# Attention and two expert layers on one core: inputs laid out ahead of the launch, soft-expert products and loads in another order

## The chip, the cores and the metric

The kernel runs on one core of a Trainium2 chip. The metric is device microseconds of one execution, the median of several runs. The engines are TensorE (PE; PEld are its weight loads), VectorE (DVE), ScalarE (ACT), GpSimd (POOL) and SyncE (SP), which here only issues DMAs. On-chip memory has 128 partitions.

## The reference

Three layers follow each other. Attention works on chunks of 32 queries with 16 keys of left context, 8 of right context and 8 memory keys per head:

```python
for c in range(nc):                       # B, H, S, D = 4, 8, 768, 64
    q_c = q[:, :, 32*c:32*c+32]
    k_full = concat([mem_k, k[:, :, 32*c-16:32*c+40]])   # cut at the ends of the sequence
    v_full = concat([mem_v, v[:, :, 32*c-16:32*c+40]])
    a = exp(s - max(s)); a = a / (sum(a) + 1e-9)         # s = scale * q_c @ k_full.T
    out[:, :, 32*c:32*c+32] = a @ v_full
# soft layer: x is [3072, 512], 8 experts with 4 slots each
logits = x @ phi
d = softmax of logits over the tokens; slot_input = d.T @ x
for e in range(8):
    slot_out[e] = relu(slot_input[e] @ w1[e]) @ w2[e]    # w1 512x1024, w2 1024x512
x = (softmax of logits over the slots) @ slot_out
# last layer: noisy top-2 of 8 experts for each token, the same shapes of w1 and w2
out = sum over the two experts of weight * (relu(x @ w1[e]) @ w2[e])
```

## The kernel before

There are three stages: attention (0 to about 153 us), the soft layer (to about 206 us) and the top-2 layer (to the end). The change is in the first two.

**Attention** (`attention`, L1067) runs 32 steps; step i = 2u + s is half s (12 chunks) of unit u, a pair of heads of one batch. The order of the work is written by hand: a loop over i for most steps, and the list ORDER (L44) for the last four together with the dispatch of the soft layer. Step i of the loop issues, in this order: scores of step i+1 (qk, L1177, 24 small matmuls), their maximum (mx, L1190), transposes of Q or K of a later unit (tr, L1153, six transposes and four ACT copies, L1163), subtraction (sub, L1198) and exponential (L1203, ACT), the shift of V (L1135), transpose of the probabilities (at, L1208) and its copy (atc, L1214, ACT), products with V of step i-1 (av, L1223), normalization (nrm), the V load of step i+3 (L1117), a zero piece of the output (L233) or a weight piece (L161), the copies of memory values (mem_rows, L1130, POOL), parts of the logits (L1260 to L1277), and a transpose of the finished tokens of step i-2 (xt, L1246) with its copy (xtc, L1253, DVE). Q and K come from memory in their own layout (L1102) and are turned on PE; `fill_mem` (L1142) puts the memory keys between them. V comes twice a step, one transfer for each head, to 32 partitions, in runs of 64 values; `shift` copies its context to the next 32 partitions, one head on DVE and one on POOL. V has four buffers, K two. Every load waits on SP's queue, which issues in order, until its buffer has been read.

**Weights of the soft layer.** Matrices 0 to 15 are w1 and w2 of the eight experts in turn, 2 MB each, loaded in four pieces of 512 KB. `home` (L142) gives each its place: 0 and 1 in two tiles of their own, the rest in the large tile `big`, whose columns also hold the attention buffers (called arena) and the tokens xs. Matrices 0 to 3 are loaded during attention (`load_piece`); 4 to 10 are issued behind it, each when its place has been read, and 11 to 15 from within the soft stage (`next_load`, L205). Behind these come the first two matrices of the last layer (`first_load`, L216), into the place of matrices 0 and 1.

**Soft stage** (`soft`, L244). For each expert: first products (L258, 16 matmuls into PSUM p1), clearing hz (POOL, L263), relu (ACT, L264), two transposes (L267), a DVE copy into hz (L268), second products (L272, accumulated over all experts in po). Behind it stands the preparation of the last stage: `bounds` (L241) reads the first w2 of the last layer, and the routing uses the soft output.

Of the kernel before, what the change touches and what calls it, by code (L numbers as in the profile page):

```python
# [19 lines left out]
NMEM = 8  # L20
# [7 lines left out]
E = 8  # L28
SL = 32
KB_W = 40 * NCH + 24  # L30
VC = 130
# [95 lines left out]
def tile_kernel(ctx, tc, q, k, v, mem_k, mem_v, phi, sw1, sw2, wg, wn, noise, mw1, mw2, cf_in, c16_in, out):  # L127
# [14 lines left out]
    home = [*raw, *home[7:9], *home[3:7], *home[0:3], *home[7:9], *home[3:6]]  # L142

    with ExitStack() as sctx:
# [28 lines left out]
        with ExitStack() as actx:  # L173
# [4 lines left out]
            attention(tc, nc, q, k, v, mem_k, mem_v, phi, xs, L, K, phis, arena, ab, wk, ps, load_piece, zero_piece)  # L178
# [17 lines left out]
        with ExitStack() as fctx:  # L196
# [47 lines left out]
def soft(tc, nc, SIT, L, C, CT, SOT, zt, table, K, K16, WT, next_load, first_load, bounds, tabs, fw, ps):  # L244
# [8 lines left out]
    for e in range(E):  # L253
        w1, w2 = WT[2 * e], WT[2 * e + 1]
        p1 = ps.tile([128, 256], F32, name="p1", bufs=1)
# [14 lines left out]
        for f in range(8):  # L270
# [3 lines left out]
            if f % 2:  # L274
                next_load(2 * e + 1, f // 2)
# [1218 lines left out]
```

## Time and profile before

| what | us |
|---|---|
| median of 3 runs | 531.72 (531.41 to 531.77) |
| profiled execution | 533.19 |
| its span, first to last instruction | 531.4 |
| PE / DVE / ACT / POOL busy | 488.7 / 323.9 / 258.7 / 260.2 |

The span is what the trace covers; the time of the profiled execution also holds what lies around it. Busy time is a sum over the three stages, so it does not say which engine limits a stage; the windows, the chain of waits (followed back from the last instruction to what released each step) and the timeline do. DMA share is the mean busy share of the 16 DMA engines and can pass 1 when packets overlap.

### The profile page before, as it was taken

Reading aid. Unit: us, or ns where it says so; the run is one execution under the profiler, and the core shown is the slowest. Engines: PE = TensorE matmul, PEld = TensorE weight load, DVE = VectorE, ACT = ScalarE, POOL = GpSimd, SP = SyncE. Lnnn points to the kernel's source line nnn. Section 1 sums busy time; section 2 is a strip of 40 time slices with the busy share of each in tenths; the row PEclk is TensorE's granted clock in tenths of the full one; section 3 lists DMA queues with packets and bytes.
Section 4 is the critical chain, followed back from the end, with each engine's and each line's share of the span. In section 5 each row is a group of like instructions: output and inputs, shape, how many; then the busy total and the mean of one; then the engine's idle time right before and its main releaser. Section 6 shows DMA issues by size and latency. Waiting matters only on the chain.

```text
span 531.4 us, 12425 instructions
## 1 busy us (share of the span) xinstructions
PE 488.7 (92%) x4854; PEld 271.2 (51%) x4854; DVE 323.9 (61%) x748; ACT 258.7 (49%) x456; POOL 260.2 (49%) x320
## 2 busy tenths in 40 slices
PE   3899998988878888999999999999999999999994
PEld 2666666766433425455454445454544544455441
DVE  6599999989852006896658665674584575552310
ACT  4788887877210206364438254273272462543221
POOL 5877887777030000553735355355336563454223
PEclk9899999999998999999999999999999999999998
DMA  9699999999999999795884939647667773353345
GB/s 201 180 243 237 239 271 241 247 231 316 407 408 358 412 410 344 228 315 169 187 257 107 285 56 222 185 98 189 178 158 166 160 202 48 43 66 44 44 56 64
DMA packets 86178, 109.89 MB, mean 207 GB/s; under 512 B 39408, under 2 KB 52656, under 8 KB 86112
## 3 DMA queue, kind: packets, MB, share of 16 engines
q1 hardware_dynamic: 76240, 93.52, 58.5%
q0 software_dynamic: 9456, 15.36, 20.3%
q8 instruction: 40, 0.66, 0.5%
q14 instruction: 26, 0.21, 0.1%
q10 hardware_dynamic: 416, 0.15, 0.1%
HBM read 88.36 MB, written 20.64 MB: 205 GB/s over the span
## 4 chain that ended last, share of the span: by engine, by line
PE 70%; DMA 14%; ACT 6%; POOL 4%; issue 3%; DVE 2%; POOLq 0%; SPq 0%; DVEq 0%; ACTq 0%
PE l L777 44%; DMA big<-in_v_dram 5%; PE l L747 4%; DMA big<-in_moe_w_dram 3%; PE tr L1153 3%; PE st L1177 3%; PE g L383 2%; ACT big L1163 2%; PE av L1223 2%; PE l L774 2%; PE po L272 2%; DMA w<-in_moe_w_dram 2%; ACT qT L1163 2%; PE p L258 2%; DMA cg<-table,idx 1%
## 5 line engine op out<-in xcount | busy, mean ns | idle before, releaser
L777 PE MATMUL l<-big,hi 128*128 128x512 f16 x768 | 174.2, 379 | 0.2 <-ACT hi L751 0.2
L802 POOL DMA_INDIRECT out_dram<-y,C x46 | 77.5, 1685 | 125.9 <-ACT ctt L709 75.7
L759 DVE SCALAR_TENSOR_TENSOR lo<-l,hi 128x1024 f16<-128x1024 f32 x50 | 61.1, 1222 | 101.5 <-ACT hi L751 101.5
L777 PEld LDWEIGHTS <-hi 128*128 128x128 f16 x768 | 72.6, 98 | 82.7 <-issue 2.9
L796 ACT ACTIVATE y<-l,gw 128x512 f32<-128x512 f32 x44 | 30.1, 685 | 137.6 <-PE l L777 133.6
L777 PE MATMUL l<-big,lo 128*128 128x512 f16 x384 | 90.7, 379 | 0.0
L777 PEld LDWEIGHTS <-lo 128*128 128x128 f16 x384 | 37.4, 98 | 43.6
L1130 POOL COPY big<-big 32x768 f32<-32x768 f32 x64 | 57.1, 893 | 3.7
L635 POOL DMA_INDIRECT cg<-table,C x44 | 46.6, 1059 | 22.0 <-issue 12.2
L751 ACT ACTIVATE hi<-l 128x1024 f16<-128x1024 f32 (+1 forms) x51 | 51.3, 1009 | 6.9 <-PE l L747 2.5
L1163 ACT ACTIVATE qT<-tr 64x384 f32<-64x384 f32 x64 | 33.8, 528 | 17.3 <-PE tr L1153 16.6
L471 DVE SCALAR_TENSOR_TENSOR big<-w,C,big 128x1024 f16<-128x1024 f32 x32 | 40.0, 1278 | 0.2
L1153 PE MATMUL tr<-cf,big 128*128 128x128 f32 x192 | 30.9, 300 | 8.4 <-DMA cf<-in_const_f_dram 4.7
L467 ACT ACTIVATE big<-w,C 128x1024 f16<-128x1024 f32 x32 | 35.6, 1149 | 3.1 <-DVE C L422 2.9
L1135 POOL COPY big<-big 24x768 f32<-24x768 f32 x32 | 27.1, 848 | 18.9 <-DMA big<-in_v_dram 17.6
L1177 PE MATMUL st<-big,qT 128*32 128x128 f32 (+2 forms) x768 | 29.6, 286 | 6.0 <-ACT big L1163 2.8
L1163 ACT ACTIVATE big<-tr 64x384 f32<-64x384 f32 x64 | 33.0, 515 | 4.1 <-PE tr L1153 3.2
L1223 PE MATMUL av<-big,aT 128*32 128x130 f32 x768 | 28.1, 279 | 3.8 <-PE at L1208 1.6
L1153 PEld LDWEIGHTS tr<-cf,big 128*128 128x128 f32 x192 | 22.5, 150 | 15.2 <-issue 5.6
L747 PE MATMUL l<-ctt,big 128*128 128x128 f16 x384 | 29.3, 219 | 0.0
L395 DVE TENSOR_REDUCE mxp<-w 128x1 f32<-128x2048 f32 x12 | 27.3, 2277 | 0.0
L1177 PEld LDWEIGHTS st<-big,qT 128*32 128x32 f32 x768 | 20.6, 114 | 12.5 <-ACT big L1163 6.0
(274 smaller groups left out, 640.1 us busy)
## 6 DMA issues: line engine op xcount, KB each, us to landing
w<-in_moe_w_dram SPq DMA_DIRECT2D x72, 512.0 KB, 7.2
big<-in_moe_w_dram SPq DMA_DIRECT2D x56, 512.0 KB, 10.0
big<-in_v_dram SPq DMA_DIRECT2D x62, 104.0 KB, 6.1
big<-in_q_dram SPq DMA_DIRECT2D x16, 384.0 KB, 6.0
big<-in_k_dram SPq DMA_DIRECT2D x16, 384.0 KB, 6.6
out_dram<-zt SPq DMA_DIRECT2D x2, 1536.0 KB, 12.4
out_dram<-zt SPq DMA_DIRECT2D x6, 384.0 KB, 5.8
out_dram<-zt SPq DMA_DIRECT2D x1, 768.0 KB, 5.3
```

Source lines behind the costliest of these rows:

```text
L471: stt(lo, w2, sc[:, rk, 5:6], hi, op0=OP.mult, op1=OP.subtract)
L635: b = nc.gpsimd.indirect_dma_start(out=CG[i][:, 32:], out_offset=None, in_=table, in_offset=bass.IndirectOffsetOnAxis(ap=icol(c), axis=0))
L747: nc.tensor.matmul(p[:, k, :], GT[i][:, 128 * k:128 * k + 128], CTT[i], start=True, stop=True)
L751: nc.scalar.activation(HI[i][:, k], p[:, k], AF.Relu)
L759: stt(LO[i].rearrange("p k t -> p (k t)"), p.rearrange("p k t -> p (k t)"), 0.0, HI[i].rearrange("p k t -> p (k t)"), op0=OP.max, op1=OP.s ...
L777: nc.tensor.matmul(P2[i], h[i][:, k, :], dyn(W2f, i, w * 4096 + 512 * k, 512, RG.get(i)), start=x == 0 and k == 0, stop=x == last and k == 7)
L802: b = nc.gpsimd.indirect_dma_start(out=out, out_offset=bass.IndirectOffsetOnAxis(ap=icol(c), axis=0), in_=y, in_offset=None, compute_op=OP ...
L1130: nc.gpsimd.tensor_copy(vcols(i, p, 32, 66 * h, D), mvs[p:p + 32, i // 2:i // 2 + 1, :].to_broadcast([32, NH, D]))
L1153: nc.tensor.transpose(p[:, y, 128 * t:128 * t + 128], RW[n % 3][:, 128 * i:128 * i + 128], identf)
L1163: nc.scalar.activation(o, i, AF.Copy)
L1177: nc.tensor.matmul(st[32 * j:32 * j + 32, g, :, w0:w1], QT[u][:, 32 * c:32 * c + 32], kb[:, :, 40 * c + w0:40 * c + w1], start=True, stop= ...
L1223: nc.tensor.matmul(p[32 * j:32 * j + 32, g, :], AT[i][:, g, 32 * j:32 * j + 32], VB[i % NV][:, c:c + 130], start=True, stop=True, tile_pos ...
```

## The change

- The inputs are given to the kernel in other layouts, made with numpy ahead of the launch: Q already transposed; K transposed, cut by chunk with the memory keys between (40 columns a chunk); V by chunk with a column of ones (13 x 65 values a partition); gate, noise weights and noise by partition.
- With them go tr, its ACT copies, the transposes of the memory keys and fill_mem. K is loaded with two transfers to 64 partitions each (246 KB), Q with one (393 KB), V with two to 32 partitions each (108 KB). K and Q have three buffers.
- In the loop the shift of the first head and xtc move from DVE to ACT (`fast`); the other head's shift stays on POOL. In ORDER both stay on DVE, and tr(31) is gone.
- The zero pieces of the output are spread otherwise, and the eighth is issued among the soft loads. Two of the four pieces of matrix 7 are loaded in attention, in steps 24 and 26; the arena leaves their place free.
- Eight matmuls of zeros stand on PE at the start.
- In the soft stage the first products and the relu of expert e+1 are issued ahead of the transposes and second products of expert e, with two p1 buffers; the loads follow that order, and some matrices have other places.

The core of the diff:

```diff
-KB_W = 40 * NCH + 24
-VC = 130
+KB_W = 40 * NCH
+VC = 65
...
-ZA = {2: (0, 1), 13: (1, 2), 17: (2, 3), 21: (3, 4), 25: (4, 5), 26: (5, 7), 27: (7, 8)}
+ZA = {5: (0, 1), 9: (1, 2), 13: (2, 3), 17: (3, 4), 19: (4, 5), 21: (5, 6), 25: (6, 7)}
...
-    home = [*raw, *home[7:9], *home[3:7], *home[0:3], *home[7:9], *home[3:6]]
+    home = [*raw, *home[7:9], *home[3:7], home[0], home[2], home[1], home[3], home[7], home[5], home[8], home[4]]
...
         def load_piece(i):
+            if i >= 16:
+                load_w(7, i - 14)
+                return
             load_w(i // 4, i % 4)
...
-            for m in range(4, 11):
-                for x in range(4):
+            for m in (4, 5, 6, 7, 8, 10, 9):
+                if m == 8:
+                    zero_out(nc.sync, out, zt, 7, 8)
+                for x in range(2 if m == 7 else 4):
                     load_w(m, x)
 
             def next_load(m, x):
-                if 2 <= m < 7:
-                    load_w(m + 9, x)
+                if x == 3:
+                    for a in {3: (12, 11), 5: (14,), 6: (), 7: (13, 15)}.get(m, ()):
+                        for y in range(4):
+                            load_w(a, y)
...
-    for e in range(E):
-        w1, w2 = WT[2 * e], WT[2 * e + 1]
-        p1 = ps.tile([128, 256], F32, name="p1", bufs=1)
+
+    def first(e):
+        w1 = WT[2 * e]
+        p1 = ps.tile([128, 256], F32, name="p1", bufs=2)
         for j in range(4):
             for g in range(4):
                 nc.tensor.matmul(p1[32 * g:32 * g + 32, :], SIT[:, j, :], w1[:, j, 256 * g:256 * g + 256],
                                  start=j == 0, stop=j == 3, tile_position=(0, 32 * g))
             next_load(2 * e, j)
         hs = fw.tile([128, 256], F32, name="hs", bufs=2)
+        nc.scalar.activation(hs, p1, AF.Relu)
+        return hs
+
+    hs = first(0)
+    for e in range(E):
+        w2 = WT[2 * e + 1]
         hz = fw.tile([128, 8, SL], F32, name="hz", bufs=2)
         nc.gpsimd.memset(hz, 0.0)
-        nc.scalar.activation(hs, p1, AF.Relu)
+        ahead = first(e + 1) if e + 1 < E else None
         pt = ps.tile([128, 2, 4, SL], F32, name="pt", bufs=1)
...
+        hs = ahead
...
+    KB = [carve(2 * KB_W).rearrange("p (h w) -> p h w", h=2) for i in range(3)]
+    QT = [carve(S)] + [wk.tile([128, S], F32, name=f"qT{i}", bufs=1) for i in range(2)]
+    HB = (NH + 1) * VC
+    VB = [carve(2 * HB) for i in range(NV)]
...
+    def load_k(u):
+        for h in range(2):
+            p = slice(64 * h, 64 * h + 64)
+            nc.sync.dma_start(KB[u % 3][p, h, :], k[u][p])
+
+    def load_q(u):
+        nc.sync.dma_start(QT[u % 3], q[u])
...
     def load_v(i):
...
         for h in range(2):
+            nc.sync.dma_start(VB[i % NV][64 * h:64 * h + 32, h * HB:h * HB + HB], v[i, h])
...
-    def tr(n):
...
-        for i in range(6):
-            y, t = (i, 0) if x == 0 else (i % 2, i // 2)
-            nc.tensor.transpose(p[:, y, 128 * t:128 * t + 128], RW[n % 3][:, 128 * i:128 * i + 128], identf)
-        for h in range(2):
-            for r in range(2):
-                i = p[64 * r:64 * r + 64]
-                if x == 0:
-                    o = custom(QT[u][64 * h:64 * h + 64], r, [[12, 64], [2, 6]])
-                    i = i[:, :, 64 * h:64 * h + 64].rearrange("p y r -> p r y")
-                else:
-                    o = custom(KB[u % 2][64 * h:64 * h + 64, h, 16 + r:], 0, [[40, NCH], [24, 2], [4, 4], [2, 2]])
-                    i = i[:, :, 192 * h:192 * h + 192].rearrange("p y (c f a) -> p c f a y", f=2, a=4)
-                nc.scalar.activation(o, i, AF.Copy)
...
+    def shift(i, fast=None):
+        nc.gpsimd.tensor_copy(vcols(i, 96, 24, 1, D), vcols(i, 64, 24, 1, D, 1, NH + 1))
+        o, x = vcols(i, 32, 24, 0, D), vcols(i, 0, 24, 0, D, 1, NH + 1)
+        if fast:
+            nc.scalar.activation(o, x, AF.Copy)
+        else:
+            nc.vector.tensor_copy(o, x)
...
+    def xtc(i, fast=None):
...
+        if fast:
+            nc.scalar.activation(XT[z][:, hp, :], p, AF.Copy)
+        else:
+            nc.vector.tensor_copy(XT[z][:, hp, :], p)
...
+    load_k(0)
+    load_q(0)
+    load_v(0)
+    load_k(1)
+    load_q(1)
+    load_v(1)
+    load_v(2)
+    load_k(2)
+    load_q(2)
+    load_v(3)
+    for h in range(2):
+        nc.gpsimd.memset(KB[0][64 * h:64 * h + 64, 1 - h], 0.0)
...
+    pw = ps.tile([128, 3, 130], F32, name="pw", tag="av", bufs=1)
+    for x in range(8):
+        nc.tensor.matmul(pw[:, 0, 0:128], zt[:, 0:128], zt[:, 128:256], start=True, stop=True)
...
         qk(n)
         mxr(n)
-        tr(i + 3)
-        if s == 1:
-            fill_mem(u + 2)
         if i == 6:
             nc.gpsimd.dma_start(phis, phi.rearrange("(j p) s -> p j s", p=128))
         sub(n)
         expo(n)
-        shift(i)
+        if i < 2:
+            clear(i + 2, nc.vector)
+        shift(i, True)
+        if i == 0:
+            mem_rows(2)
         at(i)
         atc(i)
+        if s == 0 and u + 3 < NU:
+            load_k(u + 3)
+            load_q(u + 3)
         if i >= 1:
             av(i - 1)
             nrm(i - 1)
             load_v(i + 3)
             zero_piece(i)
+            if i in (24, 26):
+                load_piece(i // 2 + 4)
         if i >= 2:
             mem_rows(i + 1)
         if s == 0:
...
+            xtc(i - 2, True)
...
+    x["q"] = x["q"].reshape(units, 2, S, D).transpose(0, 1, 3, 2).reshape(units, 128, S)
+    kt = x["k"].reshape(units, 2, S, D).transpose(0, 1, 3, 2).reshape(units, 128, NCH, 2, 16)
+    mk = x["mem_k"].reshape(units, 2, NMEM, D).transpose(0, 1, 3, 2).reshape(units, 128, 1, NMEM)
+    kb = np.empty((units, 128, NCH, 40), np.float32)
+    kb[..., 0:16] = kt[..., 0, :]
+    kb[..., 16:24] = mk
+    kb[..., 24:40] = kt[..., 1, :]
+    kb = kb.reshape(units, 128, KB_W)
+    x["k"] = kb
+    vp = np.zeros((units, 2, S + 32, D), np.float32)
...
+    vb = np.ones((units, 2, 2, 32, nh + 1, VC), np.float32)
+    for z in range(2):
+        w = vp[:, :, 32 * nh * z:32 * nh * z + 32 * (nh + 1)].reshape(units, 2, nh + 1, 32, D)
+        vb[:, z, :, :, :, :D] = w.transpose(0, 1, 3, 2, 4)
+    x["v"] = vb.reshape(2 * units, 2, 32, (nh + 1) * VC)
```

## Rows read from the trace of the kernel before

**Rows 1.** Page: busy us, share of the span and instructions.

```profile
PE 488.7 (92%) x4854; PEld 271.2 (51%) x4854; DVE 323.9 (61%) x748; ACT 258.7 (49%) x456; POOL 260.2 (49%) x320
```

**Rows 2.** Windows: busy us of PE, PEld, DVE, ACT, POOL; granted clock, DMA share, GB/s.

```profile
54.00:62.00 8.00, 7.74 (x144) 5.57 (x132) 7.32 (x20) 6.48 (x13) 6.51 (x9) 1.00 1.17 239
144.00:149.00 5.00, 4.65 (x52) 2.15 (x50) 3.57 (x8) 0.49 (x1) 0.00 (x0) 1.00 1.02 413
159.00:164.00 5.00, 5.00 (x48) 1.79 (x40) 1.92 (x4) 0.00 (x0) 0.55 (x3) 0.66 1.09 265
```

**Rows 3.** Chain of waits: start us, us, what it waited on.

```profile
46.90 13.65 DMA big<-in_v_dram x2
...
193.31 10.23 DMA w<-in_moe_w_dram
```

**Rows 4.** PE timeline, 0 to 40 us: start us, us, line, operation.

```profile
27.30 0.86 PE L1177 MATMUL st<-big,qT 128*32 128x96 f32 x24 [0.17 <-ACT big L1163]
```

**Rows 5.** Groups by form, 40 to 120 us: count, busy us, mean ns, idle before.

```profile
L1130 POOL COPY big<-big 32x768 f32<-32x768 f32 x42 | 38.3, 911 | 2.5
L1163 ACT ACTIVATE big<-tr 64x384 f32<-64x384 f32 x44 | 22.7, 517 | 2.0 <-PE tr L1153 1.3
...
L1135 POOL COPY big<-big 24x768 f32<-24x768 f32 x21 | 17.9, 850 | 12.3 <-DMA big<-in_v_dram 11.6
L1153 PE MATMUL tr<-cf,big 128*128 128x128 f32 x120 | 17.7, 282 | 1.2 <-issue 1.2
L1135 DVE COPY big<-big 24x768 f32<-24x768 f32 x21 | 15.7, 746 | 0.7
...
L1253 DVE COPY xT<-xt 128x384 f32<-128x384 f32 x21 | 11.5, 547 | 0.0
...
L1203 ACT ACTIVATE a<-a 128x384 f32<-128x384 f32 x20 | 10.5, 525 | 3.9 <-DVE a L1198 3.5
```

**Rows 6.** Timeline, 120 to 160 us: end of the loop, first soft products.

```profile
124.22 0.86 PE L1177 MATMUL st<-big,qT 128*32 128x128 f32 x24
...
125.30 0.56 DVE L1190 TENSOR_REDUCE mx<-st 128x6 f32<-128x384 f32 x1
...
125.97 0.62 DVE L1198 TENSOR_TENSOR a<-st,mx 128x288 f32<-128x288 f32 x2
...
128.06 0.86 PE L1177 MATMUL st<-big,qT 128*32 128x96 f32 x24 [0.91 <-ACT big L1163]
...
129.34 0.86 PE L1177 MATMUL st<-big,qT 128*32 128x128 f32 x24
...
154.05 1.93 PE L258 MATMUL p<-w,phis 128*32 128x256 f32 x32 [0.32 <-DVE phis L1376]
```

**Rows 7.** Timeline, 0 to 20 us: the start-up on POOL.

```profile
3.76 0.60 POOL L1385 DMA_DIRECT2D big<-in_mem_v_dram  x1 [0.47 <-DVE big L1395]
4.35 1.89 POOL L1397 MEMSET big<- 64x984 f32 x2
...
12.42 5.23 POOL L1130 COPY big<-big 32x768 f32<-32x768 f32 x6
```

**Rows 8.** Timeline, 190 to 215 us: one expert, and the last wait for weights.

```profile
190.57 0.44 PE L267 MATMUL pt<-cf,hs 128*128 128x128 f32 x2 [0.56 <-ACT hs L264]
...
191.36 1.92 PE L272 MATMUL po<-big,hz 128*32 128x512 f32 x16 [0.35 <-DVE hz L268]
...
193.10 1.91 PE L258 MATMUL p<-big,phis 128*32 128x256 f32 x32
...
195.57 0.44 PE L267 MATMUL pt<-cf,hs 128*128 128x128 f32 x2 [0.56 <-ACT hs L264]
...
203.62 1.06 ACT L241 ACTIVATE big<-w 128x1024 f32<-128x1024 f32 x1 [0.20 <-DMA w<-in_moe_w_dram]
```

**Rows 9.** Timeline of SP's DMA issues, 120 to 165 us.

```profile
128.46 34.42 SPq L161 DMA_DIRECT2D big<-in_moe_w_dram  x29
```

**Rows 10.** Page: DMA issues, count, KB each, median us to landing.

```profile
big<-in_v_dram SPq DMA_DIRECT2D x62, 104.0 KB, 6.1
```

More of the change, by code (lines that the diff above doesn't have):

```diff
@@ L126, in tile_kernel @@
 @with_exitstack
-def tile_kernel(ctx, tc, q, k, v, mem_k, mem_v, phi, sw1, sw2, wg, wn, noise, mw1, mw2, cf_in, c16_in, out):
+def tile_kernel(ctx, tc, q, k, v, mem_v, phi, sw1, sw2, wgn_in, noise, mw1, mw2, cf_in, c16_in, out):
     nc = tc.nc
@@ L1176, in qk @@
                 w1 = 56 if c == NCH - 1 else 64
-                nc.tensor.matmul(st[32 * j:32 * j + 32, g, :, w0:w1], QT[u][:, 32 * c:32 * c + 32],
-                                 kb[:, :, 40 * c + w0:40 * c + w1], start=True, stop=True,
+                nc.tensor.matmul(st[32 * j:32 * j + 32, g, :, w0:w1], QT[u % 3][:, 32 * c:32 * c + 32],
+                                 kb[:, :, 40 * c + w0 - 16:40 * c + w1 - 16], start=True, stop=True,
                                  tile_position=(0, 32 * j))
@@ L1231, in nrm @@
         rc = wk.tile([128, 3, 2], F32, name="rc")
-        nc.vector.tensor_scalar(rc, p[:, :, D:D + 2], 1.0e-9, None, op0=OP.add)
+        nc.vector.tensor_scalar(rc, custom(p, D, [[130, 3], [65, 2]]), 1.0e-9, None, op0=OP.add)
         nc.vector.reciprocal(rc, rc)
@@ L1247, in xt @@
         XP[i] = p
-    def xtc(i):
+    def xtc(i, fast=None):
         u, z = divmod(i, 2)
@@ L1376, in d_sitc @@
         nc.vector.tensor_copy(phis[:, 2 * h:2 * h + 2], M[0, h])
-    load_raw(0)
-    load_raw(1)
-    for z in range(2):
-        (nc.scalar, nc.gpsimd)[z].dma_start(mkr[:, :, z, :], mem_k.rearrange("b h m d -> (h m) b d"))
+    load_k(0)
[10 more added lines that the diff above has]
+        nc.gpsimd.memset(KB[0][64 * h:64 * h + 64, 1 - h], 0.0)
     for h in range(2):
@@ L1461, in attention @@
             xt(i - 2)
-            xtc(i - 2)
-    ops = dict(qk=qk, mx=mxr, tr=tr, sub=sub, exp=expo, at=at, atc=atc,
+            xtc(i - 2, True)
+    ops = dict(qk=qk, mx=mxr, sub=sub, exp=expo, at=at, atc=atc,
                av=lambda i: av(i, "st" if i == NI - 1 else "av"), nrm=nrm, ldv=load_v, mv=mem_rows, sp=shift, pc=load_piece, xt=xt, xtc=xtc,
@@ L1468, in attention, with arranged @@
         ops[o[0]](*o[1:])
-_INS = ["q", "k", "v", "mem_k", "mem_v", "moe_phi", "moe_w1", "moe_w2", "moe2_w_gate", "moe2_w_noise", "moe2_noise",
-        "moe2_w1", "moe2_w2"]
+_INS = ["q", "k", "v", "mem_v", "moe_phi", "moe_w1", "moe_w2", "gates", "moe2_noise", "moe2_w1", "moe2_w2"]
+def arranged(x):
+    import numpy as np
+    x = {n: np.asarray(a) for n, a in x.items()}
+    units, nh = B * HP, NCH // 2
+    x["q"] = x["q"].reshape(units, 2, S, D).transpose(0, 1, 3, 2).reshape(units, 128, S)
[8 more added lines that the diff above has]
+    vp = np.zeros((units, 2, S + 32, D), np.float32)
+    vp[:, :, 16:16 + S] = x["v"].reshape(units, 2, S, D)
+    vb = np.ones((units, 2, 2, 32, nh + 1, VC), np.float32)
[3 more added lines that the diff above has]
+    x["v"] = vb.reshape(2 * units, 2, 32, (nh + 1) * VC)
+    g = np.concatenate([x["moe2_w_gate"], x["moe2_w_noise"]], axis=1)
+    x["gates"] = g.reshape(4, 128, 2 * E).transpose(1, 0, 2).reshape(128, 8 * E)
+    x["moe2_noise"] = x["moe2_noise"].reshape(NT, 128, E).transpose(1, 0, 2).reshape(128, NT * E)
+    return x
 def kernel(**inputs):
```

116 lines of the change are left out of this document (26 added, 90 removed).

## The prediction

> **What bounds the kernel now.** I read the page's busy table first: PE is 92% busy over the span, but that is a mean over three stages [rows 1]. Cut by stage, the table of windows shows what differs. In a stretch of the attention loop PE, DVE, ACT and POOL are busy 7.74, 7.32, 6.48 and 6.51 of 8 us while the DMA engines show a share above 1 and move only 239 GB/s; at 144 to 149 us, with weights alone in flight, they move 413 GB/s at the same share [rows 2]. So in attention everything is full at once, and the DMA engines are full of something other than bytes. Then the chain of waits: inside attention it runs over V loads (13.65 us in two pieces at 46.90), and at the end of the soft stage over weight loads (10.23 us at 193.31, of "w", the first matrices of the last stage) [rows 3]. The last stage, from about 204 us on, is untouched code; it moves earlier or later as a whole. So the question is when its first load and first products are ready.
>
> I mark time by the 24-matmul score groups (qk) of the PE timeline: qk(4) starts at 27.30, qk(30) at 128.06, qk(31) at 129.34 [rows 4, 6]. That is 27.30 us of start-up, 100.76/26 = 3.875 us a step in the loop, and from qk(31), called T0, everything that follows. Three terms, one for each.
>
> **Loop, what leaves.** A step loses the six transposes of tr (17.7/20 = 0.89 us on PE) and four ACT copies at some 517 ns (2.1 us). On DVE it loses the shift of one head (746 ns) and xtc (547 ns) [rows 5]; POOL loses the fills of memory keys. ACT gains the shift, 24x768, and xtc, 128x384. ACT takes 525 ns for 384 elements from SBUF [rows 5] and 1.06 us for 1024 [rows 8]; between them 768 come to 0.85 us. So ACT does exp 0.53 + shift 0.85 + atc 0.53 + xtc 0.53 + a quarter of a logit copy 0.13 = 2.6 us; DVE 7.32 x 3.85/8 = 3.5 less 1.29, about 2.3; POOL 0.85 + 2 x 0.91 = 2.7 [rows 2, 5]. PE keeps qk, 0.86 [rows 6], av with as many matmuls, at and xt with three transposes each, half of tr's 0.89, and some 0.3 of logits: 2.9 us, which its pipelining and gaps leave at 2.8 to 2.95.
>
> **Loop, what is late next.** No engine is full, so I follow a score group through the new order on ACT (exp, shift, atc, xtc). qk to the maximum 1.08 us (124.22 to 125.30), maximum to the end of sub 1.29 (to 126.59) [rows 6], exp with hand-over 0.6, shift 0.85, atc with hand-over 0.6 [rows 5]: 4.4 us. Then on PE at 0.45, av 0.80, xt 0.45 and the logits 0.3 before the qk two steps on: 6.4 us for two steps, **3.2 us a step**. The exp waits for sub, and atc stands behind both exp and shift on ACT; PE's at and av wait for atc. That wait replaces the four copies. The trace of before has gaps marked issue in PE's stream, and a V load can be late; I add 0.15 for both and take **3.35**. Bounds: 2.95 (PE alone) and 3.75 (little gained). 26 x (3.875 - 3.35) = **13.7 us**, ends 24 and 3.
>
> **Loop, the loads.** SP's queue now carries per two steps K 2 x 246 KB, Q 393 KB, V 4 x 108 KB, one weight piece of 524 KB and some 170 KB of zeros: 2.01 MB, more than before, since the padded K is 1.25 times as large. The gain is in shape. In the attention window 1.91 MB moved in 8 us; 2.08 steps of V are 0.44 MB, the other 1.47 MB take 3.56 us at 413 GB/s, so V had 4.44 us, some 100 GB/s, if the queue never idled [rows 2]. That V went in runs of 256 bytes; now K, Q and V go in runs of 3 to 4 KB, like the weights. At 413 GB/s 2.01 MB are 4.9 us for two steps of 6.7. V(i+3) is issued after av(i-1), some 9 us ahead of its shift, and landed in 6.1 us in the fuller queue of before [rows 10]; the K and Q issued ahead of it in every second step (0.88 MB, 2.1 us) fit too. So I hold the loads at nothing in the loop; without that cover the rivals below price them.
>
> **Start-up.** Before, tr(0) to tr(2), the key-memory transposes and the four ACT copies each stood ahead of qk(0). After, qk(0) needs K(0) and Q(0), the first three transfers, there at some 6 us (V loads landed in 6.1 [rows 10], and this queue is empty). What is late next is POOL: its DMA of the value memory at 3.76 [rows 7] lands at about 8.4; six half-K clears of 0.95 us (two took 1.89) end near there too. Then mem_rows(0) and (1), four copies of 0.87 us (six took 5.23), to 11.9; shift(0) to 12.7, mem_rows(2), shift(1) to 15.3 [rows 7]. av(1) waits for that shift, and qk(4) comes after it: 16.7 in place of 27.30, **10.6 us**. Ends: 12.5 if POOL's copies run at 0.82, 8 if the first loads (3.5 MB for units 0 to 2) come at the 240 GB/s of before.
>
> **From T0 to the last stage.** Matrix 4 can be loaded only when qk(31) has read its K, before and after. Before, SP issued from 128.46 on without pause [rows 9]; 48 pieces and the 4 of the first second-layer matrix (27.3 MB, 66 us at 413 GB/s) had landed at 203.6, 74.3 us after T0, when ACT stopped waiting for them [rows 8]. The other 8 us are what stood in the queue at T0 (two pieces, zeros, the last V) and a dip to 265 GB/s at 159 to 164 us, with the granted clock at 0.66, so for most of it at the lower level, 1.2 GHz [rows 2]: the load of matrix 11 waits for the first products of expert 1, and those stood behind second products that waited for POOL. After, two pieces (half of matrix 7) are loaded in attention, one zero piece comes in, and the first products are ahead: 50 pieces and 0.39 MB, 26.6 MB, 64.4 us, and 4 to 5 us of queue at T0. Gain **5 us**, ends 1 and 7.
>
> **The reordered products** themselves I cost at nothing, because the loads hide them. From the rows: transpose 190.57, second products 191.36, first products 193.10, next transpose 195.57, 5.0 us an expert [rows 8]; without waiting for relu it is 0.79 + 1.74 + 1.75 = 4.3, six us in eight experts. First products began 24.7 us after T0 (154.05 [rows 6]), so PE could finish at T0 + 61; matrix 15 lands at about T0 + 64 and "w" at T0 + 69. If the loads were free, this edit would be worth 5 us; without the edit PE would end at T0 + 66 and just meet the loads. The smaller POOL issues (one gate load for two, noise in longer runs) leave PE's chain by 1 us and are hidden as well. Warm-up matmuls run while PE has nothing to do.
>
> **The sum.** The profiled execution took 533.19 us for a span of 531.4, 1.5 over the median of 531.72 (531.41 to 531.77). The gains are differences within that span, and I take them from the median: 531.7 - 10.6 - 13.7 - 5 = **502 us**.
>
> **Rivals.** (a) *The half-width loads set the step.* Each K load writes 64 partitions and each V load 32. The trace has no such load in long runs; its ends are 413 GB/s (long runs, all partitions) and 100 (short runs, 32 partitions). At half the weight rate, 206, 0.92 MB of K and V take 4.5 us and the rest 2.6: 7.1 for two steps, 3.55 a step, and a slower start: 26 x 0.325 + 8 + 5 = 21.5, **510 us**. For it speaks that V was late before; against it, that the two heads' loads are issued back to back and go to different partitions. The Trainium skill, "SBUF — State Buffer", section "Door 1: The DMA port swizzle", says that a transfer to partitions 0 to 63 reaches 8 of the 16 ports and so about half the rate, and speaks against this layout; no row here shows it, and by it the time would be this rival's. (b) *Slower:* K and V keep the rate that V had. At 100 GB/s they take 9.2 us of 11.9 for two steps, 5.9 a step, T0 at 172, 43 us late, less 5: about **570 us**. It decides from the point where T0 comes 5 us later than before, which is 4.47 a step, 8.9 us of loads for two, or K and V below 146 GB/s. The run length speaks against it. (c) *PE alone is the bound*, the ACT chain being overlapped better than I think: 2.95 a step, 24 us, **492 us**. (d) *The soft stage gives nothing back*: matrix 8 must wait for the last dispatch products over the first eight token tiles, 18 us after T0, and the queue gets there only at T0 + 22, so little speaks for it: **507 us**.
>
> **Chances.** Forecast 0.58 (495 to 508), (a) 0.22, (c) 0.10, (d) 0.07, (b) 0.03. What can be told from no change is about 0.2%, 1 us; only (b) and mishaps of its kind reach it: faster 0.96, same 0.01, slower 0.03. The range runs from (c) with a part of the other terms' upper ends, 489, to (a) with the low end of the soft term, 514.
>
> **What would show it.** Right: qk(4) near 17 and qk(31) near 105; the loop at 3.2 to 3.4 with DVE under 75% busy; DMA above 300 GB/s in attention; PE waiting for weights late in the soft stage and "w" landing some 69 us after T0. Wrong: idle time of ACT's shift put down to V loads (a or b); a step under 3.1 (c); loads at under 390 GB/s after T0 (d); or a last stage whose length has changed, which I take as fixed.

## The result and the profile after

The changed kernel takes **526.14 us** (median of 4 runs, 524.57 to 526.89) against 531.57 (531.36 to 531.77, 4 runs) for the kernel before: ratio 0.9899, 95% interval 0.9874 to 0.9923. It is faster, by 5.4 us (1.0%) where 29.7 were forecast, and the time lies outside the range of 489 to 514. The profiled execution took 526.89 us for a span of 525.1.

The page of the kernel after: busy us, share of the span and instructions, as in [rows 1], and the shares of the chain of waits.

```profile
PE 473.2 (90%) x4674; PEld 254.5 (48%) x4674; DVE 288.4 (55%) x689; ACT 225.0 (43%) x382; POOL 242.2 (46%) x290
...
PE 56%; DMA 32%; issue 4%; DVE 2%; ACT 2%; POOL 1%; SPq 1%; POOLq 1%; ACTq 0%
```

The work left as planned: PE is busy 15.5 us less, DVE 35.5, ACT 33.7. But 32% of the chain that ended last is now DMA (14% before). The engines were unloaded; the transfers became the bound.

The same three terms as in the prediction, by score groups on the PE timeline (start us, us, line, operation). The first line is qk(4), which answers to [rows 4]; the other two are qk(30) and qk(31), which answer to [rows 6].

```profile
19.89 0.86 PE L1148 MATMUL st<-big,qT 128*32 128x96 f32 x24
...
114.37 0.86 PE L1148 MATMUL st<-big 128*32 128x96 f32 x24
...
115.64 0.86 PE L1148 MATMUL st<-big 128*32 128x128 f32 x24
```

The end of the wait for "w" on ACT, which answers to [rows 8], and the first products of the gate on PE, the start of the last stage.

```profile
192.38 1.06 ACT L247 ACTIVATE big<-w 128x1024 f32<-128x1024 f32 x1
...
194.56 1.07 PE L397 MATMUL g<-w,SOT 128*32 128x256 f32 x16
```

| stretch | before | after | gain | forecast |
|---|---|---|---|---|
| start to qk(4) | 27.30 | 19.89 | 7.4 | 10.6 |
| qk(4) to qk(30), 26 steps | 100.76 (3.875 a step) | 94.48 (3.634) | 6.3 | 13.7 (3.35) |
| T0 (qk(31)) to "w" | 74.3 | 76.7 | -2.5 | 5 |
| "w" to the last matmuls' start | 318.06 | 318.90 | -0.8 | 0 |
| from there to the end of the span | 9.7 | 13.8 | -4.1 | 0 |

The gains add up to 6.3 us, the difference of the two spans (531.4 and 525.1). Two terms are too small, and two stretches lost what they were to keep.

Windows of the loop and of the stretch behind it in the kernel after, columns as in [rows 2], and the groups of the two halves of the shift over the whole span (count, busy us, mean ns, idle before).

```profile
20.00:114.00 94.00, 75.23 (x1462) 51.63 (x1462) 57.97 (x186) 60.28 (x111) 60.77 (x75) 0.96 1.04 279
118.00:190.00 72.00, 62.77 (x679) 29.15 (x680) 26.56 (x72) 13.02 (x26) 11.18 (x23) 0.95 1.04 399
```

```profile
L1131 POOL COPY big<-big 24x768 f32<-24x768 f32 x32 | 26.3, 823 | 34.1 <-DMA big<-in_v_dram 33.5
...
L1134 ACT ACTIVATE big<-big 24x768 f32<-24x768 f32 x28 | 23.7, 845 | 14.7 <-DMA big<-in_v_dram 14.0
```

In the loop the busiest engine, PE, works 75.23 of 94 us, the DMA engines show a share of 1.04, and they move 279 GB/s; behind the loop, with the same share, 399. Both halves of the shift stand idle for V: 33.5 us on POOL, 14.0 on ACT. Idle time of ACT's shift put down to V is the sign that the prediction gave for rivals (a) and (b), in which the loads set the step.

The same kernel again, to see how firm this is.

> The changed kernel as it is, again. It measures how far its runs spread (one profile so far) and whether the 9.4 us that POOL spends in its drain at the end come back. If that drain is a lasting part of the loss, it takes 9 to 10 us again and the time is 525 to 527; if it was chance, it is near the 6.4 us of the kernel before and the time 522 to 524.

Measured: 526.49 us (523.89 to 528.13, 4 runs), ratio 0.9924 [0.9902, 0.9947]; T0 at 113.73 and "w" at 189.89 in a span of 522.0. The medians hold within 0.4 us, while single runs spread over 4 us, so the stretches of one trace are good to about 2 us. The loss at the end was there again.

### The profile page after: what moved, and what is told of

Read it like the earlier page. It is cut to its first block, busy times and chain, and to the rows that moved or that the text cites. A ratio compares the mean times of both kernels' runs of the same rounds, so it can differ in the third digit from the quotient of the medians.

```text
span 525.1 us, 11891 instructions
## 1 busy us (share of the span) xinstructions
PE 473.2 (90%) x4674; PEld 254.5 (48%) x4674; DVE 288.4 (55%) x689; ACT 225.0 (43%) x382; POOL 242.2 (46%) x290
## 4 chain that ended last, share of the span: by engine, by line
PE 56%; DMA 32%; issue 4%; DVE 2%; ACT 2%; POOL 1%; SPq 1%; POOLq 1%; ACTq 0%
PE l L791 42%; DMA big<-in_moe_w_dram 12%; DMA w<-in_moe_w_dram 9%; DMA big<-in_v_dram 7%; PE l L761 4%; PE g L397 3%; PE l L788 2%; DMA out_dram<-y,C 2%; DMA big<-in_q_dram 1%; POOL out_dram L816 1%; ACT big L481 1%; PE tr L1310 1%; DMA cg<-table,idx 1%; POOL big L1127 1%; PE ct L721 1%
## 5 line engine op out<-in xcount | busy, mean ns | idle before, releaser
L649 POOL DMA_INDIRECT cg<-table,C x44 | 47.2, 1073 | 22.0 <-issue 11.9
L1127 POOL COPY big<-big 32x768 f32<-32x768 f32 x64 | 53.0, 829 | 4.2 <-DMA big<-in_mem_v_dram 0.5
L1131 POOL COPY big<-big 24x768 f32<-24x768 f32 x32 | 26.3, 823 | 34.1 <-DMA big<-in_v_dram 33.5
L1179 PE MATMUL at<-cf,a 128*128 128x128 f32 x96 | 18.3, 302 | 19.6 <-ACT aT L1185 17.8
L1194 PE MATMUL av<-big,aT 128*32 128x130 f32 x768 | 30.4, 293 | 2.9 <-ACT aT L1185 1.1
L1174 ACT ACTIVATE a<-a 128x384 f32<-128x384 f32 x32 | 16.8, 526 | 32.6 <-DVE a L1169 23.6
L1134 ACT ACTIVATE big<-big 24x768 f32<-24x768 f32 x28 | 23.7, 845 | 14.7 <-DMA big<-in_v_dram 14.0
L761 PE MATMUL l<-ctt,big 128*128 128x128 f16 x384 | 29.3, 219 | 0.0
L761 PEld LDWEIGHTS <-big 128*128 128x128 f16 x384 | 23.7, 98 | 6.2 <-issue 0.2
L1194 PEld LDWEIGHTS av<-big,aT 128*32 128x32 f32 x768 | 20.8, 114 | 8.9 <-issue 3.9
L1179 PEld LDWEIGHTS at<-cf,a 128*128 128x128 f32 x96 | 10.7, 147 | 27.8 <-ACT aT L1185 25.5
```

The costliest lines, as they stand in the source:

```text
L649: b = nc.gpsimd.indirect_dma_start(out=CG[i][:, 32:], out_offset=None, in_=table, in_offset=bass.IndirectOffsetOnAxis(ap=icol(c), axis=0))
L761: nc.tensor.matmul(p[:, k, :], GT[i][:, 128 * k:128 * k + 128], CTT[i], start=True, stop=True)
L1127: nc.gpsimd.tensor_copy(vcols(i, p, 32, h, D), mvs[p:p + 32, i // 2:i // 2 + 1, :].to_broadcast([32, NH, D]))
L1179: nc.tensor.transpose(p[:, g, :], A[i][:, 2 * g:2 * g + 2, :], identf)
L1194: nc.tensor.matmul(p[32 * j:32 * j + 32, g, :], AT[i][:, g, 32 * j:32 * j + 32], c, start=True, stop=True, tile_position=(0, 32 * j))
```

## The experiments

The theories. **Width:** a load that writes 64 or 32 partitions moves about half of what one that writes 128 does, and the sum of the transfers sets the loop. **Chain:** the order of work on ACT and PE takes 3.6 us a step by itself. Beside them stand the question what the soft part and the half matrix are worth, and what the end lost.

### Loads alone

```diff
+        slot = [t[:, 960 * x:960 * x + 960] for t in home[:4] for x in range(4)]
+        for u in range(16):
+            nc.sync.dma_start(slot[u][0:64], k[u][0:64])
+        for u in range(16):
+            for h in range(2):
+                nc.sync.dma_start(slot[u][64 * h:64 * h + 64], k[u][64 * h:64 * h + 64])
+        for u in range(16):
+            nc.sync.dma_start(slot[u], k[u])
+        for i in range(16):
+            for h in range(2):
+                nc.sync.dma_start(slot[i][64 * h:64 * h + 32, 0:845], v[i, h])
         with ExitStack() as actx:
```

> Four stretches of loads alone stand ahead of attention: 16 K loads to partitions 0 to 63; 32 K loads, each unit's two halves in turn; 16 K loads of a whole unit to all 128 partitions, the same runs of 3840 bytes; 32 V loads to 32 partitions, heads in turn. Width theory: 200 to 215 GB/s, the same for the halves in turn, over 400 for the whole units, and about 205 for V. Rival (the odd run lengths or the small transfers are slow): the whole units are no faster than the halves. Rival (loads were fast all along and the compute chain set the step): over 380 in all four.

Windows of the four stretches (columns as in [rows 2]): lower halves of K; the two halves in turn; whole units; V in turn.

```profile
15.00:20.00 5.00, 0.00 (x0) 0.00 (x0) 0.00 (x0) 0.00 (x0) 0.00 (x0) 0.50 1.05 207
...
45.00:50.00 5.00, 0.00 (x0) 0.00 (x0) 0.00 (x0) 0.00 (x0) 0.00 (x0) 0.50 1.04 240
...
65.00:70.00 5.00, 0.00 (x0) 0.00 (x0) 0.00 (x0) 0.00 (x0) 0.00 (x0) 0.50 1.02 419
...
80.00:85.00 5.00, 0.00 (x0) 0.00 (x0) 0.00 (x0) 0.00 (x0) 0.00 (x0) 0.50 0.94 240
```

With all loads in front the kernel took 611.72 us. K in the same runs of 3840 bytes moves at 207 GB/s to 64 partitions and at 419 to 128. Halves in turn, which is the order of `load_k`, gain little: 240, though more than the 200 to 215 expected. V to 32 partitions in turn also moves at 240, where about 205 was expected. No compute engine ran. So it is the width, not the length of the runs. Nor is it the size of a transfer, which also doubles from a half to a whole unit: V's transfers of 108 KB in turn are as fast as K's halves of 246 KB. The share is about the same, 1.02 to 1.05, at 207 and at 419 GB/s: a busy DMA engine says nothing of the rate. The Trainium skill, "SBUF — State Buffer", section "Door 1: The DMA port swizzle", has the half rate, and this run agrees (207/419 = 0.49).

### Weights and zeros behind attention

```diff
+        for i in (*range(14), 16, 17):
+            load_piece(i)
+        for i in ZA:
+            zero_piece(i)
...
-            zero_piece(i)
-            if i in (24, 26):
-                load_piece(i // 2 + 4)
...
-        if s == 0:
-            load_piece(i // 2)
```

> The weight pieces and zero pieces of the attention loop are issued behind attention instead, so the loop loads only Q, K and V: 1.32 MB in two steps for 2.01. The total gets longer, about 25 us, since the weights come later; only the loop is read. Width theory: the loads need 5.4 us for two steps, the loop falls to the 3.2 us a step of the ACT chain. Rival (the chain itself takes 3.6): it stays at 3.6.

Start of qk(4) and qk(30), and the window between (columns as above):

```profile
20.70 0.86 PE L1152 MATMUL st<-big,qT 128*32 128x96 f32 x24
...
104.32 0.86 PE L1152 MATMUL st<-big 128*32 128x96 f32 x24
```

```profile
21.00:104.00 83.00, 71.81 (x1461) 49.52 (x1450) 57.10 (x183) 60.52 (x110) 65.39 (x80) 1.00 0.78 202
```

With the queue relieved (share 0.78) the loop takes 83.62/26 = 3.216 us a step, on the 3.2 that the prediction worked out for the chain. The chain theory falls: left to itself, the new order gives what was forecast. As a kernel this is no gain (538.18 us, one run): the weights come later, "w" at 204.44 in place of 192.38; the total grew by 12 us, not by the 25 expected.

### K in one transfer

K goes to all 128 partitions at once, DVE copies the upper half to its place and POOL clears behind it.

```diff
     def load_k(u):
+        if u >= 3:
+            nc.sync.dma_start(KB[u % 3][:, 0, :], k[u])
+            return
...
+    def place_k(u):
+        kb = KB[u % 3]
+        nc.vector.tensor_copy(kb[64:128, 1, :], kb[64:128, 0, :])
+        nc.gpsimd.memset(kb[64:128, 0, :], 0.0)
...
+        if s == 1 and 3 <= u + 2 < NU:
+            place_k(u + 2)
```

> From unit 3 on K comes in one transfer to 128 partitions, the same 492 KB in the same runs; DVE copies the upper 64 partitions to their columns and POOL puts zeros back in their place, two more operations in every second step. Width theory: two steps need 5.9 us of loads for 7.1, the loop falls from 3.63 to 3.2 to 3.3 us, qk(31) comes near 107, the w loads land 12 to 15 us earlier and the time is 510 to 515. Rival (run lengths, transfer sizes) or chain theory: the step stays at 3.6 or more and the time at 524 to 528, since DVE and POOL only get more work.

Window of the loop (columns as above), and the groups of POOL's and ACT's shift and of the two new operations, 20 to 107 us.

```profile
20.00:107.00 87.00, 72.50 (x1460) 49.65 (x1455) 66.15 (x199) 60.48 (x111) 77.61 (x89) 1.00 1.01 311
```

```profile
L1142 ACT ACTIVATE big<-big 24x768 f32<-24x768 f32 x26 | 22.1, 849 | 0.6
L1139 POOL COPY big<-big 24x768 f32<-24x768 f32 x24 | 19.8, 824 | 1.5
L1120 POOL MEMSET big<- 64x960 f32 x13 | 11.6, 892 | 5.0 <-issue 3.7 <-POOL big L1135 0.6
...
L1119 DVE COPY big<-big 64x960 f32<-64x960 f32 x13 | 8.8, 679 | 0.4
```

**516.49 us** (514.0 to 518.52, 4 runs), ratio 0.9721 [0.9681, 0.9762]. The same bytes of K, 13 of 16 units at full width, are worth about 10 us, though DVE and POOL do 20 us more work. (The expectation was a little too good: 510 to 515 us, and 3.2 to 3.3 a step.) 311 GB/s in place of 279; qk(4) at 19.56 and qk(30) at 106.89, so 3.36 us a step; T0 at 108.16, "w" at 181.30 (192.38 after). An estimate from the loads alone: 26 half transfers of 245.76 KB are 6.39 MB, 26.6 us at 240 GB/s and 15.3 at 417, so 11.3 us; "w" came 11.1 earlier (8.6 against the same kernel run again). The shift no longer waits for V at all (0.6 and 1.5 us idle), although V's own loads are as narrow as before: V was late because of what stood ahead of it in the full queue, the slow K above all.

### The halves from two queues

```diff
-            nc.sync.dma_start(KB[u % 3][p, h, :], k[u][p])
+            (nc.scalar if h else nc.sync).dma_start(KB[u % 3][p, h, :], k[u][p])
...
-            nc.sync.dma_start(VB[i % NV][64 * h:64 * h + 32, h * HB:h * HB + HB], v[i, h])
+            (nc.scalar if h else nc.sync).dma_start(VB[i % NV][64 * h:64 * h + 32, h * HB:h * HB + HB], v[i, h])
```

> The changed kernel, with the second head's half of every K and V load issued from ACT's queue instead of SP's; layouts and bytes are unchanged. Alone, halves in turn on one queue moved 235 to 242 GB/s, whole transfers 414 to 419. Theory (a load on half the partitions is slow, but loads to different halves can run beside each other): with two queues the halves overlap, the attention window moves over 320 GB/s, the loop takes 3.3 to 3.45 us a step instead of 3.63, T0 comes at 107 to 110, and the time is 517 to 521 us, about as with K in whole transfers. Rival 1 (the two halves already overlap as far as they can, because one queue keeps many transfers in flight): 3.6 us a step and 525 to 527 us. Rival 2 (ACT's issues wait for buffers in ACT's stream and delay exp and the shift): over 3.7 us a step, 528 us or more.

The window of its loop:

```profile
20.00:122.00 102.00, 78.67 (x1451) 52.26 (x1440) 57.25 (x184) 60.47 (x110) 64.51 (x80) 0.95 1.02 270
```

270 GB/s, no more than the 279 from one queue; 3.96 us a step (qk(4) at 19.48, qk(30) at 122.50), 529.53 us (526.94 to 531.55), ratio 0.9953 [0.9917, 0.999]. The hope that the halves run beside each other falls a second time: rival 1 for the rate. That the step is longer than with one queue fits rival 2 (ACT issues 1.5 loads a step ahead of its own work), but how much of the 0.33 us that is was not separated. The Trainium skill says it in "SBUF — State Buffer", section "Can I just issue two DMAs to hit both halves?": no, a second transfer to the other half gained only 6% there. Alone in one queue it was more here (235 to 242 against 207 to 214 GB/s, some 13 to 16%), from two queues in the loop nothing.

### The parts of the soft stage

Old product order in the changed kernel; the loads keep their order and are tied to other products:

```diff
-                    for a in {3: (12, 11), 5: (14,), 6: (), 7: (13, 15)}.get(m, ()):
+                    for a in {3: (12,), 4: (11,), 5: (14,), 6: (13,), 7: (15,)}.get(m, ()):
...
-    hs = first(0)
     for e in range(E):
+        hs = first(e)
...
-        ahead = first(e + 1) if e + 1 < E else None
...
-        hs = ahead
```

> The changed kernel with the products of the soft stage back in their old order (each expert's second products ahead of the next expert's first), the loads in the same order as in the changed kernel. Theory (the loads set the end of that stage): the same as the changed kernel within 1 us, 525 to 527.5, though PE needs 0.7 us more an expert. Rival (the product order is what gave the gain of the change): 530 or more.

525.38 us (522.15 to 525.9), ratio 0.9872 [0.982, 0.9923].

No half matrix in attention:

```diff
-            if i in (24, 26):
-                load_piece(i // 2 + 4)
...
-                for x in range(2 if m == 7 else 4):
+                for x in range(4):
```

> The changed kernel with all of matrix 7 loaded behind attention, none of it in steps 24 and 26. Theory (the DMA queue is full from the first us to the last weight, so it does not matter on which side of qk(31) a piece goes): within 1 us of the changed kernel, with qk(31) some 2 us earlier and the w loads no later. The prediction counted 2.6 us for these two pieces: by it the time would be 528 to 530.

524.77 us (523.6 to 525.53), ratio 0.9881 [0.9842, 0.9921]; T0 at 114.38, "w" at 190.02. T0 is not the 2 us earlier that were expected: 1.3 against the first run of the changed kernel, and 0.7 later than in the second.

The kernel before with the soft part alone (products, places and load order; attention unchanged):

```diff
-            for m in range(4, 11):
+            for m in (4, 5, 6, 7, 8, 10, 9):
...
+    hs = first(0)
     for e in range(E):
...
+        ahead = first(e + 1) if e + 1 < E else None
...
+        hs = ahead
```

> The kernel before with only the soft stage changed: first products ahead, the loads and places in that order, nothing of attention. Theory: the loads from 129 us on set the end of the stage, so little is gained: 529 to 531.5, what there is coming from the 265 GB/s dip at 159 to 164 us that should go. Rival (order and loads are worth the 5 us that the prediction gave to the third term): 526 to 528.

530.29 us (529.74 to 531.32, 10 runs), ratio 0.9989 [0.9971, 1.0007].

All three agree: neither the product order nor the half matrix is worth anything that can be measured. The gain belongs to the new layouts and what goes with them in attention; the copies moved to ACT, the zero pieces and the matmuls at the start were not tried by themselves.

The dip to 265 GB/s at 159 to 164 us [rows 2] was put down to the product order, and that is not so. With the new order and the old layouts it is still there (263 GB/s at 158 to 162 us); in the changed kernel with the old order no 4 us between 126 and 186 fall below 406. With it went the old layout of the gates and the noise: in the kernel before, POOL's load of the noise, in runs of 32 bytes, is in flight when the rate falls (its packets start at 161.4 to 162.6 us). That this load is the cause was not tried by itself; the missing bytes are about 1.8 us of the full rate, an estimate ((412 - 265) x 5 / 412).

### The end of the span

POOL's scatters of the result pass a drain four token tiles ahead of the end. POOL timelines of the last stretch, before and then after (start us, us, line, operation, idle before):

```profile
519.07 0.09 POOL L800 MEMSET spacer<- 1x1 f32 x1 [4.72 <-issue]
...
524.57 1.55 POOL L802 DMA_INDIRECT out_dram<-y,C  x1 [1.31 <-ACT y L796]
```

```profile
512.62 0.09 POOL L814 MEMSET spacer<- 1x1 f32 x1 [8.03 <-issue]
...
517.09 1.55 POOL L816 DMA_INDIRECT out_dram<-y,C  x1 [0.27 <-issue]
```

Before, POOL stood 4.72 us idle in the drain, went on at 519.07 and then waited for ACT's results: the drain was hidden. After, it stood 8.03 us and went on at 512.62, behind PE's last matmuls (511.28), and three scatters followed with no wait but their own issue. The drain itself:

```profile
L1026 POOLq DRAIN  x1: 6422/6422/6422, 512.6 to 512.6; - x1
```

```profile
L1040 POOLq DRAIN  x1: 9443/9443/9443, 502.8 to 502.8; - x1
```

The first line is of before, the second of after. Without the drain (its two lines removed):

> The changed kernel without the drain that POOL waits in ahead of its last three scatters (9.4 us in the changed kernel, 6.4 us in the kernel before). If that wait is what makes the last stage longer, the scatters follow PE's last tiles as before and the time falls by 3 to 5 us, to 521 to 523. If the last three scatters wait for something else, it stays at 525 to 528.

528.7 us (10 runs, nine of them at 526.01 to 532.33 and one at 536.55), ratio 0.995 [0.9921, 0.9978]: not faster than the changed kernel, where 521 to 523 were expected. The last scatter was at 516.84 and the span ended at 530.5, 13.7 us later (8.0 in the changed kernel, 6.8 before). This fits a wait that has to happen somewhere, though the profiled run was a long one (532.33 us). Two tries at why the drain is longer, with the number of POOL's loads and that of its instructions as the suspects, both smaller in the changed kernel: the gate's and phi's loads in two parts each, and a tiny memset a step.

```diff
+        nc.gpsimd.dma_start(g2[:, 0:32], wgn_in[:, 0:32])
+        nc.gpsimd.dma_start(g2[:, 32:64], wgn_in[:, 32:64])
...
+            nc.gpsimd.dma_start(phis[:, 0:2], f2[:, 0:2])
+            nc.gpsimd.dma_start(phis[:, 2:4], f2[:, 2:4])
```

> The changed kernel with two more DMAs issued by POOL (the gates and phi in two parts each), as many as POOL issued in the kernel before. If POOL's wait in the drain at the end depends on what its DMA queue has carried, it falls from 8 us of idle time to 4.7, as before, and the last stage is 3 us shorter. If not, it stays at 8. The rest of the kernel should take the same time.

```diff
+        nc.gpsimd.memset(mq[0:1, 0, 0:1], 0.0)
         if i < 2:
+            nc.gpsimd.memset(mq[0:1, 0, 0:1], 0.0)
```

> The changed kernel with 30 tiny POOL operations more in the attention loop, as many instructions on POOL as in the kernel before. If the drain's wait at the end comes from where POOL's later instructions lie in its program, the wait falls from 8 us of idle time to 4.7. If not, it stays at 8. The loop may get up to 0.1 us a step longer.

POOL's idle time at the drain was 7.99 us in the first and 7.82 in the second (524.92 and 523.75 us, one run each): by these runs neither count sets it. It was 7.6 to 8.1 in the kernels built on the changed one in which it was read with the drain in its place, and 4.7 in the kernel before and in the one with the soft part alone. Why stays open. Where it stands can be chosen, though; in the kernel with K in one transfer it was put four tiles earlier:

```diff
-        if n == len(seq) - 4:
+        if n == len(seq) - 8:
             nc.gpsimd.drain()
```

> The kernel with K in whole transfers (516.49 us), with POOL's drain four token tiles earlier in the last stage. Theory (the drain holds back the last tiles' scatters, and PE's work hides it when it stands earlier): the last scatter starts about 1 us behind PE's end as in the kernel before, and the time falls by 2 to 4 us, to 512 to 514. Rival (the wait only moves: what the drain does not wait for has to be waited for at the end, as when it was taken out): the gap from the last scatter to the end of the span grows from 8 to 10 us or more, and the time stays at 515 to 518 us.

```profile
474.71 1.00 POOL L649 DMA_INDIRECT cg<-table,C  x1 [8.24 <-issue]
...
504.68 1.55 POOL L816 DMA_INDIRECT out_dram<-y,C  x1 [3.59 <-ACT y L810]
```

**513.74 us** (510.28 to 514.18, 4 runs), ratio 0.9645 [0.961, 0.968], the best of all; the interval just misses the 0.9681 to 0.9762 with the drain in its old place, and the single runs touch (514.0 was the shortest there). POOL still stands 8.24 us in the drain, but at 466 to 475 us, where PE has work. The last scatter now waits for ACT's result, 2.9 us behind the start of PE's last matmuls (501.79), as before (2.9), and the span ends 10.0 us behind that start (9.7 before, 13.8 after, 13.2 with K in one transfer and the drain in its old place). The rival falls: the gap from the last scatter to the end is 7.1 us and did not grow.

## Why the prediction went wrong, point by point

**The step that failed** is "So I hold the loads at nothing in the loop". It took V's 100 GB/s [rows 2] for an effect of the short runs and gave the new loads the 413 GB/s of the weights, since their runs are as long. The rows could not separate the two causes, because V was narrow and in short runs at once; I chose the run length. Both were at work in the kernel before: V in long runs moves at 240 alone, by the prediction's own estimate at some 100 in short ones. The loads alone show that width halves the rate by itself, and the reason given against rival (a), that the two halves are issued back to back to different partitions, is worth a rise from 207 to 240 GB/s, not to 419. Rival (a) had the mechanism and the price a step (3.55 forecast, 3.63 measured) and got 0.22; it should have been the forecast. It also missed the time, 510, because it moved only the first two terms.

**Loop, what leaves and what is late next: right.** ACT's shift was put at 850 ns and took 845; the chain at 3.2 us and took 3.216 once the queue was relieved. Left out was that a second limit, at 3.6, lay above it.

**Start-up: 7.4 for 10.6.** POOL's work was nearly on time: the first four copies of memory values ended at 12.3 (forecast 11.9). Yet qk(4) came at 19.89, not 16.7, because the products of step 1, which stand ahead of it, started only at 18.61. First the rows of ACT (shift and copy of step 1), then of DVE (clearing of a V buffer, normalization of step 0) and of PE (those products):

```profile
15.93 0.84 ACT L1134 ACTIVATE big<-big 24x768 f32<-24x768 f32 x1
16.80 0.49 ACT L1185 ACTIVATE aT<-at 128x384 f32<-128x384 f32 x1
```

```profile
16.50 0.76 DVE L1376 MEMSET big<- 64x845 f32 x1 [0.21 <-issue]
...
17.84 0.56 DVE L1206 TENSOR_TENSOR big<-av,rc 128x384 f32<-128x384 f32 x1
```

```profile
18.61 0.88 PE L1194 MATMUL av<-big,aT 128*32 128x130 f32 x24 [0.71 <-DMA big<-in_k_dram]
```

The copy of step 1 stands on ACT behind the shift of step 1 and the exp of step 2, which waited 1.72 us for DVE's subtraction, itself behind the clearing of V buffers. But the copy had ended at 17.29. The last thing that the products needed was the tile `av` in PSUM, where PE writes its results and of which there is only one: the normalization of step 0 on DVE reads it until 18.40, and it too stands behind the clearing. The profile puts the wait down to a K load, which these products do not read; in the run of the same kernel again it names POOL instead, while the normalization ends 0.18 us ahead of PE's weight loads in both (18.40 and 18.58, 18.08 and 18.26). I followed POOL alone and left out DVE's clears and ACT's queue, though the chain that I worked out for the loop has both engines in it.

**From T0 to the last stage: -2.5 for +5.** The term took T0 for the start of the transfers that end at "w". But the DMA engines are full on both sides of it (share 1.04 in both windows above). The first piece of matrix 4 is issued 3.1 us after T0, where it stood 0.9 ahead of T0 before [rows 9], because two pieces of weights and the loads of V(31), which before had gone out ahead of T0 as well (V(31) at 126.74), now go out behind it (start us, us, line of SP's issues):

```profile
116.07 0.94 SPq L161 DMA_DIRECT2D big<-in_moe_w_dram  x2
117.45 0.81 SPq L1122 DMA_DIRECT2D big<-in_v_dram  x2
118.73 3.19 SPq L161 DMA_DIRECT2D big<-in_moe_w_dram  x4
```

The second half of V(31), issued at 117.90, took 7.81 us to land by the chain of waits. In the 72 us from 118 to 190 the kernel after moved 399 x 72 = 28.7 MB; the kernel before moved 28.4 in the 72 us from 130 to 202. From T0 to "w" itself it was 397 x 76.74 = 30.5 MB after and 395 x 74.28 = 29.3 MB before (columns as in [rows 2]; the first two rows are of before, the third of after):

```profile
130.00:202.00 72.00, 59.16 (x719) 28.41 (x713) 26.26 (x72) 12.93 (x26) 9.26 (x19) 0.98 1.05 395
129.34:203.62 74.28, 61.44 (x749) 30.22 (x749) 28.20 (x75) 14.57 (x30) 9.86 (x20) 0.98 1.05 395
...
115.64:192.38 76.74, 65.95 (x749) 31.38 (x749) 30.35 (x80) 14.66 (x29) 13.42 (x25) 0.96 1.04 397
```

The rate was the same, so the stretch is longer because more bytes fell into it: two pieces fewer behind attention left no fewer bytes behind T0, and what they displaced was late instead. A later T0 or an earlier one, with more or fewer pieces ahead of it, changes little as long as all bytes of all shapes pass the same full queue. The run without the half matrix shows it (T0 and "w" within 2.4 us of after, and within 0.7 of the same kernel run again), and so does K in one transfer, where "w" moved 11.1 us and T0 only 7.5. So the "2 pieces less" and the "queue at T0" were terms of a sum that does not exist here; the sum that counts is that of the transfer times from the start to "w".

**The reordered products at nothing: right,** by the runs with the old order and with the soft part alone, and hidden by the loads, as said. Wrong was only that they would also remove the dip.

**The last stage "which I take as fixed": wrong by 4.9 us,** 4.1 of them behind the start of PE's last matmuls, with the drain, and 0.8 in its work, which is no more than the spread. Why the drain is longer stays open. I read its PE rows and not POOL's last 20 us; a drain whose cover is the 1.31 us that the last scatter waits for ACT should have had a price.

**The sum.** 29.3 us of terms less 3.2 (start-up), 7.4 (loop), 7.5 (T0 to "w") and 4.9 (last stage) is 6.3 us, the difference of the spans. The direction and the chance of faster held; rival (b) fell, since K and V in turn move at 240 GB/s alone and not at 100.

## What to carry to other kernels

Before a load is given the rate of another one, compare both the partitions that it writes and the length of its runs; if the trace has no load of the new width, the half rate is the forecast and the full rate the rival. Where the DMA engines are full over several stages, add up the time of all transfers up to the wait that counts; pieces moved from one side of a mark to the other gained nothing here. A wait that is hidden today, such as a drain ahead of the end, needs the length of its cover written beside it; here putting it where there is more work to hide it gained 2.8 us, and taking it out gained nothing.

## What was not expected of the hardware

- DMA share near 1 at 207 GB/s and at 419 GB/s alike: the share tells that the engines are occupied, not how well. Bytes a second by window, against the best rate seen in the same trace, tell more.
- A second half transfer adds some 13 to 16% from one queue (207 to 214 GB/s become 235 to 242) and nothing from two (279 to 270 GB/s in the loop).
- POOL's drain took 6.4 us in the kernel before and 9.4 in the changed one, at the same place of the program; the number of POOL loads and that of POOL instructions were each tried once and changed nothing.
- The granted clock was 1.00 in the loop before, with K in one transfer and with the weights behind attention, and 0.96 in the loop after: it was 0.50 there, the lower level of 1.2 GHz, at about 62 to 65 and 92 to 96 us, each time after PE had stood some 2.1 us for ACT's copy. The first of the two on PE's timeline, where products with V and a score group take 1.53 and 1.36 us for the usual 0.88 and 0.86:

```profile
61.17 0.55 PE L1179 MATMUL at<-cf,a 128*128 128x128 f32 x3 [2.13 <-ACT aT L1185]
61.65 1.53 PE L1194 MATMUL av<-big,aT 128*32 128x130 f32 x24
...
63.94 1.36 PE L1148 MATMUL st<-big,qT 128*32 128x96 f32 x24
```

  The length of the loop does not show it. Over the kernels with the same attention code, one such stretch went with 92.9 to 95.3 us from qk(4) to qk(30) (the same kernel again, the old product order, no drain), two with 93.3 to 94.5 (after, more POOL loads).
